# Fifteen loads move from SyncE's queue to ScalarE's, and every engine gets a new order

## The chip, the core and the metric

The kernel runs on one core of one Trainium2 chip. A core has five engines that run their own instruction streams: TensorE (PE) for matrix products, VectorE (DVE), ScalarE (ACT) and GpSimd (POOL) for everything that is elementwise or a reduction, and SyncE (SP), which here only issues transfers. Transfers are carried by 16 DMA engines. The metric is the device time of one execution in microseconds (us).

## What is computed

Attention with a forget gate over 8 batches of 8 heads (576 positions, head size 64), and behind it a bilinear feed-forward block over the 4608 tokens:

```python
scores = scale * np.matmul(q, k.transpose(0, 1, 3, 2))
cum = np.cumsum(np.log(np.clip(f, 0.0001, 1.0)), axis=-1)
scores = np.where(causal, -1000000000.0, scores + cum[:, :, :, None] - cum[:, :, None, :])
attn = np.exp(scores - np.max(scores, axis=-1, keepdims=True))
attn = attn / (np.sum(attn, axis=-1, keepdims=True) + 1e-09)
x = np.matmul(attn, v)          # then to (tokens, 512)
out = (x @ w_a) * (x @ w_b) @ w_out   # 512 -> 1536 -> 512
```

## The kernel before

The work is cut into numbered steps (`Op`, 2343 of them). Each step names an engine, or several to choose from, and a function that issues its instructions. A text called ORDER lists all steps by number, and a text called CHOICE gives one letter (D, A, P, S for DVE, ACT, POOL, SP) for each step that has a choice. The function `laid_out` (line 1096) reads both; the last loop calls the functions in that order. So each engine runs its steps in the order of ORDER, and an engine that has to wait for a semaphore holds up everything behind it on that engine. The costs in the `Op` calls are the planner's and are not read when the kernel runs.

Attention goes by t = 0 to 31, a pair of heads (two halves of 64 partitions), four t for each batch. For one t:

- `load_spread` (line 471) loads one row of the cumulated gate to 128 partitions, 576 KB into one of three buffers `spread`; step "bc" and the number t, from t = 8 on. POOL then masks two copies in it. For t = 4 to 7 TensorE spreads the row, and a copy out of PSUM (`spread_ev`, also called "bc") brings it to the buffer.
- `qk_group` (line 404) makes the scores in PSUM, `do_decay` (L520, DVE) adds the gate and takes the maximum, `do_exp` (L547, L551, ACT) takes the exponential, `do_norm` (L569, POOL) divides by the sum.
- `do_tr` (line 579) transposes the result with DMA transposes on SP's queue, "tr t A" and "tr t B" (L583, into PTA and PTB; for t = 4 to 7 A is cut into A0 and A1, which go into parts of xT). `do_pv` (L611) and `do_pv4` (L627) multiply them with v. From t = 8 on, the scores of t + 2 and the products with v of t are one step of TensorE, named by the scores ("qk").

The inputs of batch b come in seven loads (`load_v` line 239, `load_qk` line 252), here called by batch, tensor and part: k0 and q0, k1 and q1 (576 KB each), v0 and v2 (two transfers of 256 KB) and v4 (one of 128 KB). All go to one ring of three buffers, `n32`. POOL casts them to f16, TensorE transposes q and k through PSUM (`pe_transpose`, L278), and a copy by DVE or ACT (`pe_evict`) stores them as qT and kT.

The feed-forward block goes by chunks of 256, 256, 256, 384, then six of 512 tokens and a last one of 384. For each of 12 blocks of 128 columns TensorE makes psa and psb (L888, four matmuls each), ACT copies psa to f16 (`ff_copy`, L233), DVE multiplies (`ff_mul`, L899); then TensorE makes the output (L908), ACT or DVE copies it and SP stores it (L918). psa, psb, pso and the transposes of q and k share three PSUM buffers ("ff"): a fourth group can start only when the first has been copied. The feed-forward blocks are interleaved with attention, so that TensorE has work while attention waits.

Before the change SP's queue issues every load of q, k, v and spread, every DMA transpose and every store; POOL's issues the weights. In the first 20 us the gate is prepared on DVE and ACT (`clip` L177, LN L205, `scan` L180, a split into two f16 parts L209 and L185), while q and k of batch 0 are cast and transposed.

Of the kernel before, what the change touches and what calls it, by code (L numbers as in the profile page):

```python
# [25 lines left out]
def kernel(  # L26
# [212 lines left out]
    def load_v(b, sbs):  # L239
# [12 lines left out]
    def load_qk(b, which, half):  # L252
# [10 lines left out]
        nc.sync.dma_start(out=x.rearrange("p j t d -> p j (t d)"),  # L263
                          in_=src[:, 128 * half:128 * half + 128].rearrange("j p x -> p j x"))
# [38 lines left out]
    def batch_inputs(b, base):  # L303
# [7 lines left out]
        for n, (which, sbs, gm) in enumerate(order_):  # L311
            p = base - 50 + 3 * n
            gt = gate(gm)
            if which == "v":
                w, m = sbw[sbs[0]], len(sbs)
                ld = Op("SP", 0.58 * m, lambda _, sbs=sbs: load_v(b, sbs), gt, prio=p,
# [17 lines left out]
            ld = Op("SP", 0.58, lambda _, which=which, half=half: load_qk(b, which, half), gt, prio=p,  # L334
# [136 lines left out]
    def load_spread(t):  # L471

        nc.sync.dma_start(out=spread[t % RING["bc"]][:, :, SM:SM + S],
                          in_=cum_d[t:t + 1, :].to_broadcast([128, 2 * S]).rearrange("p (h s) -> p h s", h=2))
# [183 lines left out]
    def attention(t, base):  # L658
# [12 lines left out]
        if not direct:  # L671
# [11 lines left out]
            else:  # L683
                bc = Op("SP", 0.55, lambda _: load_spread(t), [o6] + last_bc[-1:], prio=prio(0) - 5, land=packets(128, 4608), lat="bc", name=f"bc{t}", bulk=True)
# [302 lines left out]
    for n in cuts:  # L987
# [3 lines left out]
        26 1 0 20 32 38 44 3 4 27 2 19 21 22 28 5 11 6 12 29 30 7 13 14 8 9 33 10 31 34 267 16 18 23-25 61 64  # L991
# [5 lines left out]
        235 108 236 249 85 250 95 90 127 1635-1637 1639 87 253 1641 128 1640 1638 133 1642 184 86 91 129 185 134  # L997
        130 1643 96 1644-1646 97 153 258 132 131 254 251 141 98 102 135 172 99 178 136 59 126 259 142 255 256
# [6 lines left out]
        342 1680 1681 343 1682 484 380 381 344 485 274 391 392 296 474 297 303 304 239 1683-1685 308 467 475  # L1005
        298-300 476 305 1686 324 486 1688 306 393 346 347 353 354 488 348 349 487 302 417 301 307 468 350 355
        1689 240 1690 1691 418 237 469 419 238 470 471 374 477 479 408 1693 1694 420 421 396 397 1695 1696
        411 412 356 403 1697-1700 352 337 395 351 330 394 480 357 338 310 1701 315 481 404 316 398 399 1702 483
        422 425 432 423 311 1703 426 400 1704 482 405 309 491 1687 493 360 358 1705 1706 427 433 406 312 439 440
        1707 1709 1711 435 1710 1708 1712 428 313 434 314 424 1713 442 1714 441 402 401 407 478 429 431 1715  # L1010
        1717 1718 446 447 1716 453 361 1719-1721 1723 454 443 533 448 1725 1722 449 1726 1727 496 345 494 1724
# [4 lines left out]
        547 554 414 532 531 461 462 556 1749 537 1751-1753 559 1754 1755 1757 1756 1759-1761 1758 560 1762 663  # L1016
        445 459 558 574 535 549 551 557 1763 1765 1764 542 1766 564 1767 1769 1768 1770 561 565 1771-1777 664
        543 544 658 550 1778 576 665 562 563 566-568 577 666 1779 1780 659 660 580 588 578 569 570 581 661 463
        1781 464 1783 465 1785 582 1784 1750 594 1782 587 1787 583 1788 590 1786 466 595 1789 1791 579 584 1790
        589 591 601 615 669 1745 670 592 571 572 667 683 674 1793 1795 1792 596 597 1794 598 1796 1797 602 1798  # L1020
        585 616 575 593 603 604 606 599 586 600 607 605 1799-1801 608 1802 671 609 618 610 1804-1806 619 622 630
        629 636 637 620 623 1807 624 672 632 673 611 612 668 684 675 1809 631 625 1810 639 638 681 613 614 725
        679 621 1811 1813-1815 643 1812 644 1817 617 640 633 1816 645 648 626 649 642 1819 1818 1820 646 647 627
        1821-1824 676 651 650 686 677 652 678 653 654 641 628 634 635 682 1825 1827 1829 690 1826 692 691 698
        704 1828 688 705 697 700 1831 1833 1830 693 706 1834 699 707 1835 1832 694 687 1836 701 689 856 656 655
        851 1803 1837-1839 711 708 712 1840 696 680 695 710 685 716 713 703 857 726 709 714 702 715 852 717
        1841-1843 1845 1844 1847 728 1849 1846 718 719 732 1848 720 1850 1851 1853 734 1854 722 721 730 739 733
        740 1852 1855 1856 746 747 1857 853 1858 1859 731 741 854 749 742 735 1860 858 748 859 860 729 855 863
        767 809 736 753 754 864 727 755 743 750 758 759 756 1862-1864 724 723 1808 1861 1867 770 1868 1869
        760 761 737 768 757 861 762 1865 745 763 764 774 788 776 790 751 738 752 789 791 792 782 772 775 781 794  # L1030
        744 1870 1872 1873 784 777 783 1874 1876 766 773 765 877 875 873 1877 1875 771 865 1878 866 867 1880
        1882 862 795 796 778 785 810 769 1879 800 797 801 1881 802-804 798 1883 786 793 780 799 787 779 805 806
# [5 lines left out]
        1051 912 902 904 881 1920-1922 913 1923 914-916 889 896 1047 922 926 934 940 927 933 924 941 903 897  # L1038
# [101 lines left out]
```

## Time and profile before

| | |
|---|---|
| median of 3 runs | 416.82 us (414.93 to 418.49) |
| the profiled execution | 417.89 us, of which 416.2 us are its span |
| granted TensorE clock, mean over the span | 0.995 |
| PE busy | 390.6 us, 94% of the span |
| DVE, ACT, POOL busy | 302.3, 278.1, 255.0 us |
| DMA moved | 80.58 MB, of 153432 packets 130720 under 512 B |

The span runs from the first to the last instruction of the profiled execution; 1.7 us of its time lie around it. Engine shares are averages over the whole span. These are the issues of transfers by line, with the size of one and the median time from issue to landing:

```profile
spread<-cum_d SPq DMA_DIRECT2D x24, 576.0 KB, 5.6
out_dram<-osb SPq DMA_DIRECT2D x36, 256.0 KB, 3.0
q<-in_q_dram SPq DMA_DIRECT2D x15, 576.0 KB, 5.7
k<-in_k_dram SPq DMA_DIRECT2D x15, 576.0 KB, 5.5
v<-in_v_dram SPq DMA_DIRECT2D x32, 256.0 KB, 5.5
...
PTB<-PB SPq DMA_TRANSPOSE x28, 5.3
PTA<-PA SPq DMA_TRANSPOSE x24, 4.2
...
xT<-PA SPq DMA_TRANSPOSE x8, 5.2
```

SPq is the queue that SP issues to. No transfer is issued by ACT.

### The profile page before, as it was taken

How to read it: one execution, taken by the hardware profiler on the slowest of the kernel's cores; microseconds unless marked ns; L12 is line 12 of the kernel's file. 1: busy time of each engine (PE TensorE's matmuls, PEld its weight loads, DVE VectorE, ACT ScalarE, POOL GpSimd, SP SyncE). 2: the span in 40 equal slices, each digit the busy share in tenths (PEclk: the TensorE clock that was granted, in tenths of full speed). 3: DMA queues.
4: the chain of work that ended last, by engine and by line, in shares of the span. 5: the costliest groups of instructions: out<-in, count | busy, mean ns of one | idle time of the engine just before them, and what ended most of it. 6: DMA issues, size and time to landing. Idle time of an engine off the chain costs nothing. (4 is left out here: it accounts for less than half of the span.)

```text
span 416.2 us, 10946 instructions
## 1 busy us (share of the span) xinstructions
PE 390.6 (94%) x3860; PEld 212.1 (51%) x3860; DVE 302.3 (73%) x1006; ACT 278.1 (67%) x790; POOL 255.0 (61%) x439
## 2 busy tenths in 40 slices
PE   1789999799998999999999999999999999999996
PEld 1456766566655544444444544444454444444552
DVE  5998998697777778867877889688877885342240
ACT  5886997685777578786878778677787773231231
POOL 7999898469477867686685586766856655000000
PEclk9999999899999999999999999999999999999999
DMA  8999999999999999999999999999966738200202
GB/s 261 240 217 237 184 223 224 180 234 195 243 247 224 285 246 194 275 229 273 235 229 245 251 253 196 230 215 292 213 138 165 162 63 173 95 0 2 101 2 76
DMA packets 153432, 80.58 MB, mean 194 GB/s; under 512 B 130720, under 2 KB 133280, under 8 KB 153376
## 3 DMA queue, kind: packets, MB, share of 16 engines
q1 hardware_dynamic: 149616, 75.15, 79.3%
q0 software_dynamic: 3760, 4.72, 6.9%
q8 instruction: 30, 0.49, 0.5%
q14 instruction: 26, 0.21, 0.2%
HBM read 52.05 MB, written 9.58 MB: 148 GB/s over the span
## 5 line engine op out<-in xcount | busy, mean ns | idle before, releaser
L520 DVE CUSTOM_DVE_ANT_0 S<-sc,spread 64x576 f32<-64x576 f32 (+4 forms) x232 | 124.9, 562 | 10.6 <-ACT PA L551 3.1
L888 PE MATMUL psb<-xT,wb 128*128 128x512 f16 (+2 forms) x528 | 116.1, 343 | 0.4 <-ACT a L233 0.4
L888 PE MATMUL psa<-xT,wa 128*128 128x512 f16 (+2 forms) x528 | 115.8, 342 | 0.3
L899 DVE TENSOR_TENSOR ht<-psb,a 128x512 f16<-128x512 f32 (+2 forms) x132 | 77.4, 589 | 34.0 <-PE psb L888 30.6
L233 ACT CAST a<-psa 128x512 f16<-128x512 f32 (+2 forms) x132 | 66.2, 502 | 51.6 <-PE psa L888 43.5
L551 ACT ACTIVATE PA<-S,st 128x256 f16<-128x256 f32 (+2 forms) x168 | 84.1, 503 | 24.2 <-DVE st L520 22.6
L908 PE MATMUL pso<-wout,ht 128*128 128x512 f16 x432 | 98.5, 379 | 0.0
L569 POOL TENSOR_SCALAR PA<-PA,st 128x384 f16<-128x384 f16 (+2 forms) x192 | 89.8, 480 | 12.4 <-DVE st L561 11.0
L569 POOL TENSOR_SCALAR PB<-PB,st 128x512 f16<-128x512 f16 (+1 forms) x96 | 67.5, 712 | 30.1 <-DVE st L561 16.4
L888 PEld LDWEIGHTS <-wb 128*128 128x128 f16 x528 | 50.1, 98 | 41.3 <-issue 1.3
L888 PEld LDWEIGHTS <-wa 128*128 128x128 f16 x528 | 49.4, 98 | 40.8 <-issue 1.8
L908 PEld LDWEIGHTS <-ht 128*128 128x128 f16 x432 | 40.6, 98 | 46.7 <-issue 0.5
L551 ACT ACTIVATE PB<-S,st 128x512 f16<-128x512 f32 x56 | 40.1, 717 | 11.7 <-DVE st L520 7.7
L410 PE MATMUL sc<-kT,qT 64*128 64x256 f16 (+5 forms) x480 | 43.7, 277 | 3.3 <-ACT PA L551 1.5
L551 ACT ACTIVATION_READ_ACCUMULATOR PA<-S,st 128x1 f32 x168 | 31.9, 190 | 0.0
L561 DVE RECIPROCAL st<-st 128x2 f32<-128x2 f32 x128 | 18.5, 158 | 18.2 <-ACT PB L551 13.1
L410 PEld LDWEIGHTS <-qT 64*128 64x128 f16 (+1 forms) x480 | 17.0, 98 | 28.2 <-issue 18.5
L486 POOL TENSOR_SCALAR_AFFINE_SELECT spread<-spread 128x256 f32<-128x256 f32 x24 | 9.8, 408 | 35.1 <-DVE st L520 35.1
L237 DVE CAST xT<-pv 128x512 f16<-128x512 f32 (+1 forms) x40 | 23.0, 575 | 8.8 <-PE pv L611 8.6
L547 ACT ACTIVATE PB<-S,st 128x576 f16<-128x576 f32 x28 | 21.8, 777 | 9.9 <-issue 6.5
L233 ACT COPY osb<-pso 128x512 f32<-128x512 f32 x19 | 10.9, 575 | 24.3 <-DMA out_dram<-osb 12.8
L520 DVE CUSTOM_DVE_ANT_1 S<-sc,spread 128x256 f32<-128x256 f32 x48 | 19.6, 420 | 9.4 <-PE sc L627 4.7
(85 smaller groups left out, 427.6 us busy)
## 6 DMA issues: line engine op xcount, KB each, us to landing
spread<-cum_d SPq DMA_DIRECT2D x24, 576.0 KB, 5.6
out_dram<-osb SPq DMA_DIRECT2D x36, 256.0 KB, 3.0
q<-in_q_dram SPq DMA_DIRECT2D x15, 576.0 KB, 5.7
k<-in_k_dram SPq DMA_DIRECT2D x15, 576.0 KB, 5.5
v<-in_v_dram SPq DMA_DIRECT2D x32, 256.0 KB, 5.5
wout<-in_moe_w_out_dram POOLq DMA_DIRECT2D x3, 512.0 KB, 6.4
v<-in_v_dram SPq DMA_DIRECT2D x8, 128.0 KB, 4.9
wa<-in_moe_w_a_dram POOLq DMA_DIRECT2D x2, 512.0 KB, 8.6
```

The source lines that it names most:

```text
L233: nc.scalar.copy(out=out_, in_=in_)
L237: VEC[e].tensor_copy(out=out_, in_=in_)
L410: nc.tensor.matmul(out=dst, lhsT=lhsT, rhs=rhs, start=start, stop=stop, skip_group_check=True)
L486: nc.gpsimd.affine_select(out=x, in_=x, compare_op=mybir.AluOpType.is_ge, fill=NEGBIG, base=0, pattern=[[0, 2], [-1, 128]], channel_multip ...
L520: nc.vector.tensor_tensor_reduce(out=o, in0=x, in1=y, scale=-1.0, scalar=3e38, op0=ADD, op1=MIN, accum_out=m)
L547: nc.scalar.activation(out=p_blocks(t, 4), in_=T[("s" if direct else "z", t, 4)], func=EXP, bias=st[:, 8:9], scale=sign, accum_out=st[:, 1 ...
L551: nc.scalar.activation(out=p_blocks(t, i)[:, :, h, :], in_=(T[("s", t, i)][:, h, :] if direct else T[("z", t, i)][:, h * n:h * n + n]).rea ...
L561: nc.vector.reciprocal(out=st[:, 20 + 2 * i:22 + 2 * i], in_=st[:, 10 + 2 * i:12 + 2 * i])
L569: VEC[e].tensor_scalar(out=p, in0=p, scalar1=st[:, c:c + 1], scalar2=1.0, op0=MUL, op1=MUL)
L888: nc.tensor.matmul(out=p[:, 0:n], lhsT=w16[:, db, 128 * fb:128 * fb + 128], rhs=xTflat[db][:, t0:t0 + n], start=(db == 0), stop=(db == 3))
L899: nc.vector.tensor_tensor(out=ht[:, 0:n], in0=T.pop(("psb", t0, fb))[:, 0:n], in1=T.pop(("a16", t0, fb))[:, 0:n], op=MUL)
L908: nc.tensor.matmul(out=o, lhsT=T[("ht", t0, fb)][:, 128 * tb:128 * tb + 128], rhs=wout16[:, fb, :], start=(fb == 0), stop=(fb == 11))
```

## The change

The three load functions take an engine and issue from that engine's queue. The steps of batch 1 and later (for k, q and v) and of t = 8 and later (for spread) may choose their engine, with ACT as one choice. The new CHOICE puts 15 of them on ACT and none on POOL: spread of t = 9, 12, 13, 17, 23, 26 and 29, and the loads k0, q1 and v4 of batch 3, k0 of batch 5, k0, q0 and v4 of batch 6, and q0 of batch 7. No DMA transpose and no store moves.

```diff
+    QUEUE = {"SP": nc.sync, "ACT": nc.scalar, "POOL": nc.gpsimd}
+
+    def load_v(e, b, sbs):
...
-            nc.sync.dma_start(out=t32[0:w, n],
-                              in_=v[b, :, 128 * sb:128 * sb + w, :].rearrange("h s d -> s h d"))
+            QUEUE[e].dma_start(out=t32[0:w, n],
+                               in_=v[b, :, 128 * sb:128 * sb + w, :].rearrange("h s d -> s h d"))
...
-                ld = Op("SP", 0.58 * m, lambda _, sbs=sbs: load_v(b, sbs), gt, prio=p,
+                ld = Op(None, {"SP": 0.58 * m} | ({"ACT": 0.72 * m + 0.1} if b else {}),
+                        lambda e, sbs=sbs: load_v(e, b, sbs), gt, prio=p,
...
-            ld = Op("SP", 0.58, lambda _, which=which, half=half: load_qk(b, which, half), gt, prio=p,
+            ld = Op(None, {"SP": 0.58} | ({"ACT": 0.8, "POOL": 0.68} if b else {}),
+                    lambda e, which=which, half=half: load_qk(e, b, which, half), gt, prio=p,
...
-                bc = Op("SP", 0.55, lambda _: load_spread(t), [o6] + last_bc[-1:], prio=prio(0) - 5, land=packets(128, 4608), lat="bc", name=f"bc{t}", bulk=True)
+                bc = Op(None, {"SP": 0.55, "ACT": 0.8, "POOL": 0.68}, lambda e: load_spread(e, t), [o6] + last_bc[-1:], prio=prio(0) - 5, land=packets(128, 4608), lat="bc", name=f"bc{t}", bulk=True)
...
     CHOICE = """
-        PDPPPPAADAADPDADAPDAPPPDDDDDAADDDDDDDDADAAADAADDDDDAAAAAAADADAAAADAAAAADDAAAAAAAAAAAAAADDAAAADAAADDA AAA
+        DPPPDPAADDADPPDAPPDDPPDDADDDAADDDDDDDDASAASAASSDASDASSDAAAAAAASAASADSSADSAAASSSASSAAASDASSDAADDSAAASS
+        SDDSADSSAASADSSSASSADASDAASSAASAASSSSSAADAAAASSAASDASASASSAASAAADDSSAASAASSSASS
     """
```

ORDER is replaced as a whole. What differs in it, by engine:

- TensorE: 96 of its 528 steps stand at another place, most of them one or two places off; 74 of the 96 are among the first 165 steps (roughly the first 110 us), 22 behind.
- 24 steps other than the loads change engine. Of batch 0: the first half of k's cast goes from POOL to DVE, the second part of q's first cast from ACT to DVE, the second part of k1's cast from DVE to POOL, the first part of q1's from ACT to POOL, and v4's from POOL to DVE. Three copies of spread rows (t = 4 and 5) go from DVE to ACT. From batch 3 on, six copies of transposed q and k go from ACT to DVE, one the other way.
- DVE starts with the clip of the second half of the gate (which waits for the gate's load) ahead of its casts of q; before, it cast q first.
- SP's transposes keep their sequence but for exchanges of neighbours (tr8A ahead of tr8B, for one); loads and stores move between them.

More of the change, by code (lines that the diff above doesn't have):

```diff
@@ L250, in cast_v, with load_qk @@
         cast(e, nv[b % 2][0:w, sbs[0]:sbs[0] + n].rearrange("p n h d -> p n (h d)"), t32[0:w, 0:n], False)
-    def load_qk(b, which, half):
+    def load_qk(e, b, which, half):
         if b == 0 and half:
@@ L262, in load_qk @@
         src = src_of[which][b].rearrange("(j h) (g t) d -> j (h g) (t d)", j=2, t=TG)
-        nc.sync.dma_start(out=x.rearrange("p j t d -> p j (t d)"),
-                          in_=src[:, 128 * half:128 * half + 128].rearrange("j p x -> p j x"))
+        QUEUE[e].dma_start(out=x.rearrange("p j t d -> p j (t d)"),
+                           in_=src[:, 128 * half:128 * half + 128].rearrange("j p x -> p j x"))
     def cast_qk(e, b, which, half, lo, hi):
@@ L469, in spread_tail, with load_spread @@
         nc.gpsimd.memset(spread[t % RING["bc"]][:, :, SM + SF:SM + S], 0.0)
-    def load_spread(t):
-        nc.sync.dma_start(out=spread[t % RING["bc"]][:, :, SM:SM + S],
-                          in_=cum_d[t:t + 1, :].to_broadcast([128, 2 * S]).rearrange("p (h s) -> p h s", h=2))
+    def load_spread(e, t):
+        QUEUE[e].dma_start(out=spread[t % RING["bc"]][:, :, SM:SM + S],
+                           in_=cum_d[t:t + 1, :].to_broadcast([128, 2 * S]).rearrange("p (h s) -> p h s", h=2))
     def mask_copy(t):
@@ L1016 @@
[L1016 to L1020, printed above, removed]
@@ new lines @@
+        226 60 221 287 263 288 222 264 472 231 232 385 335 384 1671 323 194 233 1673 1672 334 1675 373 293
+        339 340 329 1674 386 266 381 281 473 295 336 331 380 388 294 330 338 389 390 484 234 1676 341 1677 1679
+        342 1680 1681 1678 195 343 1682 274 485 392 391 474 1683-1685 303 296 393 297 475 298 299 304 300 476
+        417 387 301 302 1686 305 324 239 240 306 307 467 308 468 344 486 346 347 353 488 348 354 487 1688-1690
[5 rows of a table added]
+        1724 498 1725-1727 499 505 1728 506 512 513 456 450 1729 500 1730 501 1731 1733 1735 365 1734 507 1736
@@ new lines @@
+        366 1732 508 497 437 444 534 430 438 457 452 445 509 519 520 495 510 415 1737 1739 1741 489 359 514 515
+        662 573 1742 490 502 416 1738 524 525 1740 521 522 526 527 363 536 1743 516 538 528 552 553 545 539 364
+        451 530 511 523 517 518 503 504 540 409 458 1692 460 657 1746-1748 547 541 546 548 1744 531 461 462 537
+        413 1751 1749 559 554 555 1752 1753 1755 1757 1756 549 560 1754 556 542 1758 1759 529 532 1760 561 1761
+        1763 1764 414 1762 1765 1767 1768 535 663 564 562 1766 1769 551 544 669 459 667 558 557 1770 543 550 658
@@ new lines @@
+        574 1771 1773 566 1772 1774 565 1775-1777 664 576 1778 665 567 666 577 568 580 659-661 582 569 563 1779
+        463 1780 1781 594 587 570 464 581 1782 588 578 1783 465 1785 1787 1784 583 1789 590 589 1788 595 1786
+        579 1791 1793 597 1792 584 1790 466 591 601 1794 596 598 602 1745 615 571 674 1795 1796 603 683
+        1797 1798 572 1750 585 670 586 593 575 606 607 604 616 592 600 1799-1801 671 609 1802 608 672 618 610
+        622 629 1804-1806 630 636 620 637 623 1807 624 632 673 631 605 599 612 611 668 1809 625 1810 638 639
[3 rows of a table added]
@@ new lines @@
+        700 707 856 656 655 851 1803 1835 689 1836 694 711 1837-1839 712 1840 726 682 685 696 695 713 708 714
[3 rows of a table added]
+        768 727 758 743 759 750 1862-1864 760 761 1867 770 1868 1869 738 737 745 756 757 762 764 763 774 772 788
[3 rows of a table added]
+        1887 1888 1890 825 832 1889 826 819 833 815 1892-1894 1891 837 834 820 838 839 827 1895 1896 1898 1900
+        876 811 842 808 807 1866 868 843 813 1897 844 845 1899 1901-1903 840 836 874 828 821 919 880 884 891
+        1045 841 835 822 829 869 1904 882 898 899 846 885 892 848 847 886 1905 1906 1908 1910 893 900 894 1909
@@ new lines @@
+        887 901 1907 895 1911 883 870 905 902 872 881 888 906 871 1050 1871 1912 1914 1916 1913 1918 1917 907
+        1915 896 903 1051 879 897 904 1046 889 910 1919 911-913 849 850 1920-1922 1047 1923 920 914 915 890 922
+        1048 926 934 940 961 916 962 1049 1055 928 924 941-943 936 927 908 909 933 935 929 944 946 1925-1927
+        1052 925 1053 1928 947 930 931 1054 937 948 949 921 952 953 950 923 939 945 954 955 938 932 1056 951
+        1930 1931 1924 917 918 1929 1932 1935-1937 964 1940 956 1938 1933 1942 966 968 975 982 969 983 976 958
[9 rows of a table added]
@@ new lines @@
+        1134 1135 1118 1128 1117 1110 1109 1091 1097 1083 1098 1084 1156 1247 1248 1122 1129 1123 1998-2001 1241
+        1119 1242 1130 1137 1243 1136 1251 1997 1112 2003-2005 1111 2008 2010 1141 1142 1115 1143 1138 1146 1124
+        1147 2006 1131 1148 1149 2009 1150 1152 1126 2012 1158 2011 1144 1162 1160 1145 1133 1151 1197 1139 1125
+        1163 2013 2014 1159 2015 1140 1252 1132 1164 2016 2018 1176 2017 1165 2020 1170 1177 1169 1178 1171 2021
+        1179 2022 2019 1172 1166 2023-2025 1256 1265 1266 1161 1253-1255 1154 1183 1184 1180 1257 1168 1157 1198
@@ new lines @@
+        1182 1167 1153 1249 2026 2027 1188 1189 1173 1175 1181 1174 2028 2029 1185 2030 2031 1186 1258 1200 1259
+        1191 1190 1260 2032 2034 2036 1204 1202 1192 1212 1205 1211 1218 1219 1201 1187 1193 1206 1263 2033
+        1207 1208 2035 1194 2037 1214 1213 1203 1215 1225 2038 2039 1250 2040-2042 2044 2046 2002 1307 1195 1196
+        2007 1261 1226 1220 1221 2043 2048 1222 1216 1199 1230 2045 1227 1308 1224 1217 1223 1209 1231 1228 2047
+        1232 2049 1233 1234 2050 1268 2052 2051 1272 1286 1287 1279 1280 1270 1269 1274 2053 1288 2054 2055 1264
@@ new lines @@
+        1229 1236 1235 1273 1281 1289 1275 1438 1282 2056-2059 1290 1210 1292 1433 1271 1293 1294 1262 1267 1291
+        2061 1238 1237 2060 1349 1295 2062 2063 1283 1276-1278 1285 1434 1298 1296 1299 2064 1301 1300 1302 1303
+        1284 1297 1304 2066-2069 1435 1310 1312 1314 1315 1328 1322 1329 1321 1311 1439 1350 2065 1443 1316
+        1436 1437 2071-2073 1440 1313 2074 1331 1317 1324 1330 1323 1441 2076 2077 1442 1335 1336 2078 2080
[5 rows of a table added]
+        2113 2070 1445 1387 1375 1390 1389 1412 1406 1396 1399 1395 1405 1413 1401 1408 2114 1446 1407 2116-2118
[3 rows of a table added]
@@ new lines @@
+        1432 1431 2133 1448 1543 2128 2134-2136 1487 1488 1461 1502 1489 1492 1493 1484 1494-1496 1490 1449 2139
+        1504 2140 2141 1472 1477 1486 1491 1497 1505 1508 1522 1479 1498 1544 1478 1471 1485 1516 1523 1515 1509
+        1506 2137 1510 2144 1525 1518 1511 2145 1517 1524 2146 1507 2142 2147 1529 2148-2150 2152 2154 1500 1499
[4 rows of a table added]
+        1596 1580 1597-1599 2181 1574 1603 1594 1604 1610 2182 1611 2183 2184 1605 1612 2185 1606 1613 1600 1561
+        2186 1595 1607 1569 1575 1582 1581 1555 1602 1609 1570 2187 1617 1562 1563 1618 2188-2190 1614 2191 1619
@@ new lines @@
+        1601 1591 1622 1620 1616 1615 1608 1624 1623 1625 1626 1593 2192 2193 1584 1583 1629 2194 2195 1627 1621
+        1628 2197 2198 1587 2199 1588 2202 1585 2203 2204 2200 1586 2207 1630 2196 2201 2205 2208 1631 2209 1632
+        2210 2206 2211-2214 2216 2218 2215 2217 2219-2224 2226 2228 2225 2227 2229-2232 2234 2233 2235 2236 2238
+        1633 2237 2239-2242 1634 2243-2246 2248 2249 2247 2250-2252 2254 2253 2255 2256 2258 2260 2261 2257 2259
+        2262 2265-2268 2270 2263 2269 2264 2271 2272 2275 2273 2276-2278 2274 2280 2282 2281 2284 2283 2286 2285
@@ L1094 @@
+        SDDSADSSAASADSSSASSADASAASSAASAASSSSSAADAAAASSAASDASASSASSAAADDSSAASAASSSASS
     """
```

65 lines of the change are left out of this document (6 added, 59 removed), and 82 rows, old and new, of the table ORDER.

## The prediction

> **What bounds the kernel now.** I read the slices of the page first, to see whose time it is.
>
> ```profile
> PE   1789999799998999999999999999999999999996
> ...
> PEclk9999999899999999999999999999999999999999
> DMA  8999999999999999999999999999966738200202
> ```
>
> One slice is 10.4 us. PE stands at 9 from about 145 us to its last matmul: what that part takes is TensorE's own work, and the change adds no work there. Only the start (the first two slices), the stretch from 60 to 145 us and one dip of the clock (eighth slice of PEclk) can give anything back. The tail is fixed: the timeline has the last output matmul end at 412.2 us, then a copy and a store to 416.2. So the question is how long PE idles before 145 us, and whether anything new stops it later. The waits of PE say for whom it idles:
>
> ```profile
> PE psT L278 <- DVE q L235: 5.4, 1, 5.4
> PE pv L611 <- DMA xT<-PA: 3.5, 3, 2.5
> PE psT L278 <- POOL k L237: 3.2, 2, 2.8
> PE pv L611 <- DMA PTA<-PA: 1.7, 2, 1.0
> ...
> PE psT L278 <- DVE ht L899: 1.4, 1, 1.4
> ...
> PE pv L627 <- DMA PTB<-PB: 0.5, 1, 0.5
> ...
> PE psb L888 <- ACT a L233: 0.4, 1, 0.4
> ```
>
> Columns: us in total, times, longest. The first and third are the start. Behind it, the waits for a transpose are the large ones: 3.5 + 1.7 + 0.5 = 5.7 us; asked stretch by stretch, these six lie at 69, 71, 81, 97, 107 and 140 us, none later. ACT, which is to get the loads, hardly holds PE: 0.4 us for the copy of psa. The longest of them has a price beyond itself, by the windows of 1 us (PE busy, PEld, DVE, ACT, POOL, then the granted clock, DMA share, GB/s):
>
> ```profile
> 79.00:80.00 1.00, 0.00 (x0) 0.00 (x0) 0.59 (x2) 0.00 (x0) 0.80 (x1) 1.00 1.28 287
> 80.00:81.00 1.00, 0.01 (x2) 0.01 (x2) 0.00 (x0) 0.56 (x1) 0.00 (x0) 0.77 1.12 152
> 81.00:82.00 1.00, 1.00 (x9) 0.70 (x10) 0.00 (x0) 0.26 (x2) 0.00 (x0) 0.50 1.12 290
> 82.00:83.00 1.00, 1.00 (x7) 0.69 (x6) 0.40 (x1) 0.00 (x0) 0.00 (x0) 0.50 0.99 207
> 83.00:84.00 1.00, 1.00 (x7) 0.70 (x6) 0.94 (x4) 0.56 (x2) 0.00 (x0) 0.53 1.16 231
> ```
>
> After 2.5 us of idle PE runs at half clock for 2.9 us: 1.5 us more, 4.0 in all. By the Trainium skill, "TensorE: Matmul & The Clock Gate", section "Why this matters for your kernels", gaps beyond about 3 us drop the clock; here 2.5 was enough, so I go by the row.
>
> Why are the transposes late? The timeline of SP's queue (start, us it took to issue):
>
> ```profile
> 71.90 5.21 SPq L583 DMA_TRANSPOSE PTB<-PB  x1
> 77.21 1.76 SPq L583 DMA_TRANSPOSE xT<-PA  x1
> 79.06 0.54 SPq L473 DMA_DIRECT2D spread<-cum_d  x1
> ...
> 118.66 6.68 SPq L583 DMA_TRANSPOSE PTA<-PA  x1
> ```
>
> The transpose that PE wants at 81 us is the one issued at 77.21, behind one whose issue took 5.21. Adding the pieces, SP issues during 59.5 of the 63 us from 62 to 125 (94%), and 111 of the 190 us from 160 to 350 (58%). A transpose takes 1.2 to 6.7 us to issue (median 1.8), though the DMA share is at 1.05 to 1.19 in every 20 us up to 220: the engines are full too, not only the queue.
>
> **The loads leave SP.** Six of the 15 lie in the full stretch: bc9, k0, q1, v4 of batch 3, bc12 and bc13. Their issues on SP took 0.54, 0.58, 0.47, 0.65, 0.82 and 0.95 us, 4.0 in all. The bytes stay, at nearly the same place among TensorE's steps (bc9 12 steps earlier, the others within 3). What the queue gives back wait by wait: the two at 69 and 71 us (0.8) come before any moved load: nothing. At 81 us (pv5), SP's sequence ahead of the transpose is as it was, but one psb of 256 tokens now stands ahead of pv5, which covers 0.44; bc9, now issued before and not behind that transpose, could take it away again. At 97 (0.72) one spread and one store fewer stand ahead: half, 0.36. At 107 (1.0) tr8A now goes before tr8B and without k0 ahead: all of it. At 140 (0.67) bc13 is gone but two loads remain ahead: half, 0.34. Sum 2.1; bounds: 7.2 (all 5.7 and the half clock) and -4.0 (a new wait like that at 81). I take 2.1, as the engines' share says that most of the lateness is bytes. By the Trainium skill, "DMA: Bandwidth & Descriptors", section "Issuing engines are not separate DMA queues", another issuing engine saves only sequencer time, since all transfers share the 16 engines; the ceiling would then be the 4.0 us of issue rather than 7.2. The full DMA slices agree with it.
>
> **The loads come to ACT.** No row has a transfer issued by ACT. Nearest are SP's issues of the same loads: 0.36 to 2.45 us for spread (mean 0.71), 0.37 to 3.03 for q and k (mean 0.70). Behind the issue in ACT's order stand exponentials and the copies of psa, which free the three PSUM buffers for PE. Cover: in the chunks of 256 tokens a group takes 0.44 us and the copy 0.37, so a copy may come 2 x 0.44 - 0.37 = 0.5 late; with 384, 2 x 0.65 - 0.475 = 0.8; with 512, 2 x 0.864 - 0.577 = 1.15. The six loads above fall in chunks of 256 and 384, the other nine in 512. At 0.7 with exponentials close by I charge the six 0.25 each, 1.5 us, and the nine nothing. Bounds: 0, and 15 x 0.7 = 10.5 if the cover is gone everywhere. Each load also waits on ACT for its buffer. For most, the last reader stands over 40 steps earlier; close are k0 of batch 5 (a POOL cast 7 steps before), bc29 (9) and v4 of batch 3 (14).
>
> **Other choices from batch 3 on.** Five net copies of q and k leave ACT (0.63 each) for DVE (0.75): 3.8 us more on DVE, spread over some 100 us in which it is busy 14 to 18 of every 20. No gain, as ACT isn't PE's bound; cover on DVE 2 us or more per 20; without it, at most 3.8. I take 0.
>
> **The start.** Here the new order can be followed by hand.
>
> ```profile
> 4.83 0.49 DVE L235 TENSOR_SCALAR q<-q 128x512 f16<-128x512 f32 x1 [2.57 <-DMA q<-in_q_dram]
> 5.82 1.02 DVE L177 TENSOR_SCALAR cum_f<-cum_f 96x256 f32<-96x256 f32 x2 [0.49 <-DMA cum_f<-in_f_dram]
> 11.89 1.02 DVE L494 TENSOR_REDUCE st<-sc 128x2 f32<-128x512 f32 x2
> ```
>
> DVE now begins with a clip, which cannot start before 5.82, and casts q behind it. Up to the first maximum it has, by the rows: clips 0.72 + 0.38, q 0.50 and, scaled by columns, 0.62, likewise k 0.70, scans 0.67 + 0.88, splits 0.80 + 0.55 + 0.42, one copy of qT 0.75: 7.0 us from 5.82, so 12.8 against 11.89. POOL gets k1 and q1 casts between the splits (0.84 each): q1 is ready at about 15.8, and its transposes stand in TensorE's order ahead of the next scores, which began at 14.79 and now at about 16.6; the step after, at 16.38 before, follows at some 17.3. I charge 1.0; bounds 0 (the full DVE and ACT of 40 to 60 us then get 2 us less on DVE, as spread copies go to ACT) and 1.8.
>
> **Sum.** On the profiled execution: 417.9 + 1.0 + 1.5 - 2.1 = 418.3. It lay 1.1 above the median, so 417.2 for the median.
>
> **Rivals.**
>
> 1. *The queue was the limit* (faster). If transposes are late because loads stand ahead in SP's queue and not for bytes, all waits behind 71 us and the half clock go: 5.7 - 0.8 + 1.5 = 6.4, and ACT's price stays in its cover: 417.9 + 1.0 - 6.4 = 412.5, 411.4 in the median; without the start's loss 410.4. For: SP 94% full exactly where PE waits. Against: DMA share above 1.
> 2. *ACT waits for SP's issue* (slower). If the two queues' issues exclude each other, a load on ACT meets SP issuing in 94% of cases early and 58% late, and waits half of a median issue of 1.8 us before its own 0.5: 1.4 us. Over the cover (0.5 and 1.15) this is 0.9 x 6 x 0.94 + 0.25 x 9 x 0.58 = 6.4 us for PE: 417.9 + 1.0 + 6.4 - 1.1 = 424.2, if the transposes gain nothing. It decides once a load stays over 1 us on ACT. For: SP's own issues grow to 6.7 us. Against: no row shows two queues at once. The Trainium skill, "Perfetto Trace Analysis", section "DMA Instruction — HWDGE (DVE, Sync)", says that the generator of descriptors is locked for exclusive use during an issue; this trace cannot show whether across queues.
> 3. *A new long wait* (slower): bytes of ACT's queue now compete with SP's transposes, the old waits stay, and one more is as long as that at 81 us, 4.0 with the half clock: 417.2 + 2.1 + 4.0 = 423.3. For: bc9 now comes before the transpose of pv5. Against: the order of TensorE leaves most transposes as much lead as before.
> 4. *Nothing moves but the order*: the loads are issued where they were, bytes bind, and only the start is lost: 417.9, within the forecast's range.
>
> **How the numbers follow.** My forecast with rival 4: 0.35, nearly all within 1% of 416.8 (412.7 to 421.0; the three runs of before spread over 0.9%, so less than 1% is little to tell from no change): 0.30 within, 0.02 faster, 0.03 slower. Rival 1: 0.30, of which 0.26 faster, 0.04 within. Rival 2: 0.23, 0.21 slower, 0.02 within. Rival 3: 0.12, 0.10 slower, 0.02 within. So faster 0.28, within 0.38, slower 0.34. The forecast's own range is 413 to 421; with rival 1 down to 409.5 and rival 2 up to 425.5 about 0.2 is left out.
>
> **What would show it.** Start: the first maximum on DVE at 12.8 and not 11.9. Loads: rows of ACT's queue with a mean near 0.7 (over 1.0 speaks for rival 2), and PE's wait for ACT's copy at 1 to 2 us, not 0.4. Transposes: PE's waits for DMA at 3 to 4 us, the half clock still there; both gone means rival 1. SP's share from 62 to 125 us should fall to about 88%. PE waiting for ACT or DVE behind 160 us would make the prediction wrong.

## The result, and the profile after

The change makes the kernel slower: 423.91 us (median of 4 runs, 422.77 to 424.94) against 416.80 (4 runs) on the same chip, a ratio of 1.016, 95% interval 1.0125 to 1.0195. The profiled execution took 422.77 us, its span is 421.1, 4.9 more than before. All ratios below are to the kernel before on the same chip, with 95% intervals, and leave disturbed runs out; three of the profiles below (e4, e6, e13) are of longer executions than their medians, with TensorE waiting 2.4 to 4.9 us for weights near 35 us, and are used only for single transfers and waits, not for their length.

The slices of the page of after, to be laid beside those of before:

```profile
PE   1789998759989999999999999989999999999996
...
PEclk9999999969999999999999999999999999999999
DMA  8799999998999999999999999996977827300102
```

PE is again full from about 145 us on. The loss lies ahead: the eighth and ninth slices (73.7 to 94.8 us) read 7 and 5, where before they read 7 and 9, and the dip of the clock has moved to the ninth. The waits of PE in after (us in total, times, longest):

```profile
PE psT L280 <- DVE q L235: 7.9, 1, 7.9
PE pv L615 <- DMA xT<-PA: 7.6, 3, 6.3
PE sc L414 <- ACT PA L555: 1.7, 3, 0.8
PE pv L615 <- DMA PTB<-PB: 1.5, 1, 1.5
...
PE pv L615 <- DMA PTA<-PA: 0.9, 1, 0.9
...
PE pso L912 <- ACT osb L233: 0.4, 1, 0.4
```

Lines have moved by four (L611 is now L615, L583 is L587). The waits for a transpose were 5.7 us in all and are 10.0. Asked stretch by stretch, those of before at 97 and 140 us are gone and that at 107 has shrunk from 1.0 to 0.2; that of pv5 has grown from 2.5 to 6.3 (82 to 88 us), and two are new (1.5 near 124 us, 0.9 near 278). The windows of 1 us about the long one (PE, PEld, DVE, ACT, POOL, then clock, DMA share, GB/s):

```profile
81.00:82.00 1.00, 1.00 (x10) 0.68 (x7) 1.00 (x5) 1.00 (x6) 1.00 (x2) 1.00 0.26 61
82.00:83.00 1.00, 0.05 (x1) 0.00 (x0) 0.99 (x4) 0.26 (x2) 1.00 (x3) 1.00 1.44 178
83.00:84.00 1.00, 0.00 (x0) 0.00 (x0) 0.97 (x3) 0.00 (x0) 1.00 (x2) 1.00 1.22 97
84.00:85.00 1.00, 0.00 (x0) 0.00 (x0) 0.15 (x1) 0.00 (x0) 0.30 (x1) 0.88 0.85 186
...
87.00:88.00 1.00, 0.00 (x0) 0.00 (x0) 0.00 (x0) 0.20 (x1) 0.00 (x0) 0.50 1.26 199
88.00:89.00 1.00, 0.65 (x7) 0.42 (x8) 0.07 (x1) 1.00 (x3) 0.00 (x0) 0.50 1.27 290
```

PE stands, then DVE, ACT and POOL run dry behind it, and the clock is halved from about 84.8 us until about 91.6. At 81 to 82 us, where tr5B has been issued, tr5A0 is being issued and neither has landed, the DMA engines are busy at 0.26. So here it is not bytes that the transposes wait for. The lull alone isn't what is new: at 77 to 78 us in before the share was 0.46 with 30 GB/s, and in e3 below it is 0.13 with 43 GB/s at 78 to 79 us, also with tr5B not yet landed. What differs is what comes after it. SP's queue at that place (start, us to issue), then ACT's one transfer there:

```profile
74.33 0.39 SPq L477 DMA_DIRECT2D spread<-cum_d  x1
74.82 3.57 SPq L587 DMA_TRANSPOSE PTB<-PB  x1
78.47 3.66 SPq L587 DMA_TRANSPOSE xT<-PA  x1
82.23 5.41 SPq L587 DMA_TRANSPOSE PTB<-PB  x1
```

```profile
75.78 0.39 ACTq L477 DMA_DIRECT2D spread<-cum_d  x1
```

ACT's load is bc9 (the spread load of t = 9), issued 0.96 us into SP's issue of tr5B, with 2.6 us of that issue still to come; tr5A0, which pv5 waits for, follows at once. From the trace's landings and packets, beside those of before:

```
               before                         after
tr5B           71.90 issued, 80.34 landed     74.82 issued, 87.70 landed
tr5A0          77.21 issued, 80.95 landed     78.47 issued, 88.31 landed
bc9            79.06 issued, 83.94 landed     75.78 issued, 87.52 landed   (SP before, ACT after)
```

ACT is done with the issue after 0.39 us, but the first packet of its queue starts at 82.05, when SP's issue of tr5A0 ends (82.13). From there to 86 us the 256-byte packets of SP's queue come at 56 to 436 per us; in e3 below, in which these two transposes run undisturbed, they come at 1051 and 1022 per us (79 to 81 us). All three transfers land together, 10 to 13 us after their issue.

How late TensorE is against before, by the start of the same feed-forward matmul in both traces (a count from the traces, us):

```
at (before)   33    77    86    101   131   181   290   412
after         2.5   3.1   7.4   6.3   5.4   4.2   5.6   5.0
```

So 2.5 us were lost before 33 us and 4.3 more at pv5; 3.2 came back by 181 us, where before had its own waits from 97 to 140 us; 1.4 went again by 290 us.

Two more lines of the page of after, the issues by queue with the median time to landing:

```profile
spread<-cum_d SPq DMA_DIRECT2D x17, 576.0 KB, 5.6
...
spread<-cum_d ACTq DMA_DIRECT2D x7, 576.0 KB, 7.9
```

The same load takes 2.3 us longer to land from ACT's queue, in this kernel's mixture of places.

### The profile page after: what moved, and what is told of

It reads as the page before. It is cut to its first block, busy times and chain, and to the rows that moved or that the text cites. A ratio compares the mean times of both kernels' runs of the same rounds, so it can differ in the third digit from the quotient of the medians.

```text
span 421.1 us, 10948 instructions
## 1 busy us (share of the span) xinstructions
PE 391.6 (93%) x3860; PEld 212.3 (50%) x3860; DVE 304.0 (72%) x1009; ACT 277.7 (66%) x787; POOL 253.9 (60%) x439
## 5 line engine op out<-in xcount | busy, mean ns | idle before, releaser
L524 DVE CUSTOM_DVE_ANT_0 S<-sc,spread 64x576 f32<-64x576 f32 (+4 forms) x232 | 125.0, 562 | 10.1 <-PE sc L414 4.9
L573 POOL TENSOR_SCALAR PA<-PA,st 128x256 f16<-128x256 f16 (+2 forms) x192 | 89.5, 479 | 18.9 <-DVE st L565 15.1
L237 DVE CAST xT<-pv 128x512 f16<-128x512 f32 (+1 forms) x40 | 23.1, 576 | 12.8 <-PE pv L615 12.7
L615 PEld LDWEIGHTS <-nv 128*64 128x64 f16 x640 | 19.6, 110 | 17.7 <-issue 10.1
```

Source lines behind the costliest of these rows:

```text
L237: VEC[e].tensor_copy(out=out_, in_=in_)
L524: nc.vector.tensor_tensor_reduce(out=o, in0=x, in1=y, scale=-1.0, scalar=3e38, op0=ADD, op1=MIN, accum_out=m)
L573: VEC[e].tensor_scalar(out=p, in0=p, scalar1=st[:, c:c + 1], scalar2=1.0, op0=MUL, op1=MUL)
L615: nc.tensor.matmul(out=o[HP[h], 128 * i:128 * i + 128], lhsT=vt[:, j, pr + NP * h, :], rhs=pt[:, base_blk[i] + 2 * block_at(t, i, j) + h, ...
```

## The experiments

The two theories that the first four kernels were to tell apart: **A**, a load on ACT's queue that falls into SP's issue of a DMA transpose holds up both (queue and place together); against it, that the new order alone, the fifteen issues on ACT by their number, or the new start is what costs. In the diffs, 533 is bc9, 493 bc8, 360 tr5B, 358 tr5A0, 410 tr6B, 405 and 603 exponentials of t = 6 and t = 10, 674 the load q1 of batch 3, 683 bc12.

**e1: the new order, all loads on SP.**

```diff
 CHOICE, the fifteen moved loads, at their new places in ORDER
-A
+S
```

> The new order with all 15 loads issued by SP, at the places that they have in the new order. Theory A (the queue: spread of t = 9, issued early by ACT, is carried beside tr5B and tr5A0 and holds them up): PE's wait for the transpose of pv5 falls from 6.3 us to below 3 and the half clock shortens, so about 419 to 420 us. Theory B (the order: start and sequence make the wait, whoever issues the loads): the wait stays at 5 us or more and the time at 422 to 425.

**e2: the old order, the fifteen loads on ACT.**

```diff
 CHOICE of before, the fifteen loads, at their old places in ORDER
-S
+A
```

> The old order and the old choices, but the 15 loads issued by ACT at their old places, where spread of t = 9 comes behind tr5A0. Theory A with the early issue as its condition, and theory B: 416 to 418, as before. If loads on ACT cost by themselves (PE waiting for ACT's copies), 420 or more, with PE's waits for ACT above 3 us where they were 0.9 behind the start.

**e3: after, with bc9 alone at another place,** still on ACT.

```diff
 ORDER of after
-491 1687 493 360 533 1706 1707
+491 1687 493 360 1706 1707
-1721 1723 410 449
+1721 1723 410 533 449
```

> The changed kernel with one step moved: spread of t = 9, still on ACT, behind tr6B in the order and so behind six more exponentials and four more copies on ACT. Theory A: tr5B and tr5A0 land some 5 us after their issue and not 10 to 13, PE's wait falls from 6.3 us to 3 or less, and the time to 419 to 420. Theory B: the wait stays, 423 to 424.

**e4: the first 130 steps in the old order and on the old engines,** the rest as after.

> The changed kernel with its first 130 steps (to about 20 us) in the old order and with the old choices, the rest in the new order. The first maximum on DVE comes back from 13.3 to 11.9 us and the first psa from 35.5 to about 33.5. If the late start is carried to the end: 421.5 (2.4 less). If idle time behind absorbs it: 423.5. By theory A the wait for pv5 stays at about 6 us; by theory B it may fall with the start.

Measured:

```
            median (runs)    ratio   95% interval      longest wait for a transpose
after       423.91 (4)       1.016   1.0125 to 1.0195  6.3, xT, 82 us
e1          419.11 (10)      1.006   1.003  to 1.0094  2.8, PTB
e2          424.51 (4)       1.018   1.013  to 1.023   5.4, PTB, 116 us
e3          416.82 (10)      0.999   0.9954 to 1.0026  1.5, PTB
e4          423.45 (4)       1.014   1.0093 to 1.0193  7.5, xT, 86 us
```

e3 moves one step of 2343 and gives the whole loss back: 7.1 us in the medians, 2 to 3 us more than theory A expected. In its trace ACT issues bc9 at 80.99, when SP is just ending tr6B's issue, and the load lands at 86.12, after 5.1 us. The waits of PE in e3:

```profile
PE pv L615 <- DMA xT<-PA: 2.0, 3, 1.1
...
PE pv L615 <- DMA PTB<-PB: 1.5, 1, 1.5
...
PE pv L615 <- DMA PTA<-PA: 0.9, 1, 0.9
```

The wait at pv5 is down to 1.1 and the granted clock is 1.00 from 79 to 92 us. e1 says that the new order by itself costs 2.6 us, and that with SP as the issuer bc9's early place makes no such wait: at pv5 it is 2.4 us. e4 gives nothing back that can be measured: the start isn't the loss. (It also moved the weights' loads, and its profile has TensorE wait 3.4 us for them, so as a price of the start it is no more than that.)

e2 was the surprise. In the old order bc9 stands behind tr5A0, and pv5 waits only 1.2; the loss is the same size, but at another load. The queue of SP, and what ACT issued beside it:

```profile
108.56 4.67 SPq L587 DMA_TRANSPOSE PTB<-PB  x1
113.28 4.19 SPq L246 DMA_DIRECT2D v<-in_v_dram  x2
```

```profile
109.47 0.37 ACTq L477 DMA_DIRECT2D spread<-cum_d  x1
...
109.95 0.41 ACTq L265 DMA_DIRECT2D q<-in_q_dram  x1
```

bc12 and q1 come 0.9 and 1.4 us into SP's issue of tr9B. Their first packets start at 113.75, half a microsecond behind its end, and they land 10.75 and 12.26 us after issue; PE waits for that transpose:

```profile
PE pv L615 <- DMA PTB<-PB: 5.4, 1, 5.4
```

The same pattern with other steps, then, in another order. The next kernels took it apart.

**e5: the order of before, bc9 alone on ACT and early.**

```diff
 ORDER of before (and CHOICE: bc9 from S to A)
-405 309 491 1687 493 360 358
+405 309 491 1687 493 533 360 358
-443 533 448
+443 448
```

> The order and the choices of before, with one step changed: the spread load bc9 is issued by ACT behind the exponential of t = 6 (at about 74.4 us), while SP issues tr5B (71.9 to 77.1 in before). All other loads stay on SP. Theory A (a load on ACT's queue that is issued while SP issues a DMA transpose starts its packets only when that issue ends, and then both crawl): bc9 and tr5A0 land 10 us or more after their issue, PE waits 5 us or more for xT at about 82 us with the half clock behind it, 420.5 to 424 us. Rival (it takes the full set of loads on ACT, or the new order with its earlier bc9): 416 to 418 us, PE's longest wait for xT stays near 2.5.

**e6: the order of before, bc9 early but on SP,** between the two transposes.

```diff
 ORDER of before
-493 360 358
+493 360 533 358
-443 533 448
+443 448
```

> The order and the choices of before, with bc9 still on SP but one place earlier: between tr5B and tr5A0. Theory A: SP issues it by itself, so nothing crawls; tr5A0 is issued some 0.6 us later, 416.5 to 418.5 us, wait for xT at 81 us between 2.5 and 4. Rival (the place of the bytes ahead of tr5A0 is what costs, on whichever queue): 420 us or more, with a wait for xT of 5 us or more.

e5: 421.70 us (4 runs from 419.65 to 433.82; without the longest, 419.96), 1.0123 (1.0046 to 1.0201). e6: 419.34 (10), 1.0048 (1.0013 to 1.0083). ACT's issue of bc9 in e5 and SP's queue about it:

```profile
73.69 0.39 ACTq L477 DMA_DIRECT2D spread<-cum_d  x1
```

```profile
72.53 3.10 SPq L587 DMA_TRANSPOSE PTB<-PB  x1
75.72 2.77 SPq L587 DMA_TRANSPOSE xT<-PA  x1
78.60 5.96 SPq L587 DMA_TRANSPOSE PTB<-PB  x1
```

bc9's first packet starts at 78.57, again with the end of tr5A0's issue (78.49). bc9 lands 10.8 us after its issue, tr5B 12.2 and tr5A0 9.5. Of PE's waits in e5 between 79 and 92 us there is one:

```profile
PE pv L615 <- DMA xT<-PA: 5.4, 1, 5.4
```

With the profile of e2, in which bc9 is on ACT at its old place, this gives pv5's wait for all four combinations:

```
bc9        old place (behind tr5A0)   early (beside or between the transposes)
on SP      2.5 (before)               2.3 (e6), 2.4 (e1)
on ACT     1.2 (e2)                   5.4 (e5), 6.3 (after)
```

The two of the new order are e1 and after, the others of the old. Neither the queue nor the place does it; the two together do. In time e6 was 1 to 3 us dearer than expected, and the intervals of e5 and e6 overlap, so it is the waits that tell them apart, and of the times the pair after and e3.

**e7: e2 with bc12 and q1 of batch 3 some 17 steps later.**

```diff
 ORDER of before (CHOICE as in e2)
-592 571 572 667 683 674 1793
+592 571 572 667 1793
-616 575 593 603 604
+616 575 593 603 683 674 604
```

> The order of before with the fifteen loads on ACT (the kernel that measured 424.51), but bc12 and q1 of batch 3 are issued by ACT some 17 steps later, behind the exponentials of t = 10, when SP should have ended the issue of tr9B. Theory A: the wait of 5.4 us for PTB at 120 us goes and the time falls to 416 to 419.5 us. Rival (fifteen issues on ACT cost by their number, wherever they fall): 423 us or more.

**e10: e2 with these two back on SP,** at the places of before.

```diff
 CHOICE of e2, bc12 and q1 of batch 3
-A
+S
```

> The order of before with thirteen of the loads on ACT; bc12 and q1 of batch 3 stay on SP at their places of before (with all fifteen on ACT this order measured 424.51; with these two some 17 steps later it measured 421.42, but ACT then issued them at 112.73 and 113.21, at the very end of SP's issue of tr9B, 109.08 to 113.13, and its runs lay between 417.1 and 423.9). Theory A (these two cost what that kernel lost): 416 to 419 us, and no wait of 2 us or more for PTB near 120 us. Rival (it takes no particular load; thirteen issues on ACT cost by their number): 421 us or more.

Both expectations failed in time: e7 took 421.42 (10 runs from 417.08 to 423.88), 1.0085 (1.0048 to 1.0122), and e10 423.44 (4), 1.0159 (1.0124 to 1.0193). The profiled execution of e7 took 417.20 us, near the lowest of its runs, and has no wait over 1.0 us for a transpose; what the longer ones wait for isn't seen. bc12 was issued at 112.73, 0.4 us ahead of the end of tr9B's issue, so that the separation hung on a fraction of a microsecond. e10's trace is plain. SP's queue (x2 stands for two transposes), ACT's load beside it, and ACT some 12 us later:

```profile
92.63 10.02 SPq L587 DMA_TRANSPOSE PTB<-PB  x2
```

```profile
92.84 0.43 ACTq L265 DMA_DIRECT2D k<-in_k_dram  x1
```

```profile
105.07 0.77 ACT L551 ACTIVATE PB<-S,st 128x576 f16<-128x576 f32 x1 [1.85 <-DMA PTB<-PB]
```

Here k0 of batch 3 has fallen into the first transpose's issue (3.84 us of the 10.02), 0.2 us behind its start. It lands after 11.9 us and the transpose after 12.3, at 104.96. The exponential that needs the transpose's source buffer back waits 1.85 us on ACT, the copy of psa queues behind it, and PE waits for that copy:

```profile
PE psb L892 <- ACT a L233: 2.1, 2, 1.7
```

Later v4 of batch 3 falls into the issue of tr10B in the same way (1.25 of its 4.18 us are over), that transpose lands after 10.1 us, and PE waits 2.1 us for PTB near 133 us; v4 itself took only 7.0 us.

In e2 k0 at the same place was issued 0.09 us ahead of that transpose (91.60 against 91.69) and landed after 5.7 us. So what was wrong in the expectation was not the mechanism but that two named loads carry it: in the old order several of the fifteen lie at the edge of a transpose's issue, and small shifts decide which one falls in. The rival, that ACT pays by the number of loads, has the time of e10 right, but e3 and the next kernel have all fifteen on ACT at 416.8 and 415.5.

Over all fourteen profiles, in the stretch from 60 to 160 us, the 39 of 47 loads on ACT whose landing the traces give, by what was left of SP's running transpose issue when ACT issued them (a count from the traces):

```
left of the issue       loads   us from issue to landing
2.3 us or more            6     7.0, 10.7, 11.7, 11.9, 12.3, 13.0
under 2.3 us             14     4.1 to 7.5, and one of 10.8 (e5, a second transpose directly behind)
no transpose in issue    19     4.4 to 7.4
```

The bound of 2.3 us was chosen with these numbers in sight. Transposes with a load of ACT in their issue landed after 7.5 us in the median (16 of them, the slowest 13.8), the others after 5.2 (229, three quarters of them within 6.3, the slowest 10.9: tr5B of e13 below, with a load of POOL in its issue). A transpose whose issue is long both lands late and is likelier to meet a load. So among those with 3 us or more of issue: 7 with a load of ACT landed after 12.2 us in the median (7.1 to 13.8), 59 without after 7.2. Behind 160 us no load on ACT took over 9.8 us, and PE's queue of feed-forward work covers it but for 0.9 us in after (2.1 in e11).

**e9: after with three edits:** bc9 as in e3, q1 of batch 3 out of tr9B's issue, and q's casts on DVE ahead of the clip that waits for the gate.

```diff
 ORDER of after (besides that of e3)
-26 0 1 20 32 38 44 3 11 4 27 28 5
+26 0 1 20 32 38 44 3 27 28 11 4 5
-615 571 674 1795 1796 603 683 1797
+615 571 1795 1796 603 683 674 1797
```

> The kernel after the change with three edits: bc9 behind tr6B (as in the run that measured 416.82), q1 of batch 3 behind bc12 (out of SP's issue of tr9B), and DVE casts q ahead of the clip that waits for the gate's load. Theory A with a start that costs about 1 us: 414 to 415.8 us, so under both kernels; the wait of 1.5 us for PTB near 120 us goes, and the first maximum on DVE comes at about 12 us. Rival (the start's order is hidden by the full DVE and ACT from 40 to 60 us, and the wait for PTB moves elsewhere): 416 to 418 us.

**e12: the order of e9, all loads on SP.**

```diff
 CHOICE of e9, the fifteen loads
-A
+S
```

> The order of the kernel that measured 415.54 (all three edits), with the fifteen loads on SP at the same places. If the queue's time is worth what the prediction gave it (4.0 us of issue in the full stretch, of which 2.1 reach TensorE at most): 416.5 to 418.5 us. Rival (what the kernel gains over the one before comes from the order alone): 414.5 to 416.3 us.

**e11: e9 with the first 130 steps of before.**

> The first 130 steps in the order and with the engines of before; behind them the order after the change with bc9 behind tr6B and q1 of batch 3 behind bc12. If the new start costs the 1.0 to 1.5 us by which TensorE lags at 33 us in the run that measured 415.54: 413.5 to 414.8 us, under both kernels. Rival (the full engines of 40 to 60 us take it back, or the old start holds up the weights' loads): 415.5 to 418 us.

```
            median (runs)    ratio   95% interval
e9          415.54 (10)      0.998   0.9956 to 1.001
e12         419.48 (8)       1.007   1.0043 to 1.0095
e11         416.20 (12)      0.996   0.993  to 0.9991
```

ACT's two loads in e9 and SP's transpose ahead of them:

```profile
114.09 0.39 ACTq L477 DMA_DIRECT2D spread<-cum_d  x1
...
114.60 0.41 ACTq L265 DMA_DIRECT2D q<-in_q_dram  x1
```

```profile
109.53 4.37 SPq L587 DMA_TRANSPOSE PTB<-PB  x1
114.00 0.53 SPq L922 DMA_DIRECT2D out_dram<-osb  x1
```

Both now come behind the issue, land after 4.5 and 7.2 us, and the wait for PTB (1.5 in e3) is gone; PE's waits for transposes add up to 3.1 us. In e12, with the same order and SP as the issuer, that wait is back:

```profile
PE pv L615 <- DMA PTB<-PB: 2.4, 1, 2.4
```

e9 against e12 is the price of the queue with the order held fixed: 0.9%, or 3.6 us (1.0069 - 0.9983, times 416.8), in favour of ACT; by the two intervals about 2 to 5 us. The expectation of e12 failed: 419.48 lies above both of its ranges, so the queue's time is worth more than the sum gave it. So the change's move of loads does bring something once no load falls into a transpose's issue, and the new order takes 0.6 to 0.7% back (e1, e12). e9 and e11 are 1.8 and 2.0% faster than after. Against before, e11 is 0.1 to 0.7% faster by its interval, which is at the edge of what can be told; the interval of e9 contains 1. The old start makes no difference between the two that can be measured.

**e13: the order of before, bc9 alone on POOL's queue.**

```diff
 ORDER of before (and CHOICE: bc9 from S to P)
-441 402 401 407
+441 402 533 401 407
-443 533 448
+443 448
```

> The order and the choices of before with bc9 alone moved to POOL's queue, issued at about 75 us, while SP issues tr5B and tr5A0 (the same load on ACT at 73.7 us measured 421.70, on SP between the two transposes 419.34). If any second queue does it: 420.5 us or more, a wait for xT of 5 us or more at 82 us, bc9 landing 10 us or more behind its issue. If it is ACT's queue alone: 416 to 419.5 us, the wait for xT at 3 us or less.

418.28 us (10 runs from 415.21 to 422.96), 1.0012 (0.9978 to 1.0046). POOL was late and issued bc9 at 78.79, 0.7 us ahead of the end of tr5B's issue, and not in its midst. In the profiled execution, 422.96 us long, tr5B landed after 10.9 us and PE waited 5.0 for xT; the median says that this is not the rule. Whether any second queue does what ACT's does stays open.

## Why the prediction came out as it did

The forecast was 417.2 us, with a range of its own of 413 to 421 and, with the rivals, of 409.5 to 425.5; its likeliest case was no change (0.38). The time lies outside the forecast's own range and inside the wide one, as slower (0.34). Of the cases named, rival 3 came nearest, which had been given 0.12; so the wide range held, and the sum did not.

- **What bounds the kernel** was right: TensorE's idle time ahead of 145 us decided, and behind it no more than 1.4 us were lost. The sign that was to make it wrong, PE waiting for ACT or DVE behind 160 us, came to 0.9 us in all (0.2 before).
- **The transposes, -2.1: the step that failed, at one of its terms.** "At 81 us (pv5)" the sum took a gain of 0.44, and added that bc9, "now issued before and not behind that transpose, could take it away again". It took away far more: the wait went from 2.5 to 6.3, so this term is +3.8 where -0.44 stood. I had seen that bc9's place was new, gave it nothing in the sum, and kept it for the bound and for rival 3, as bytes ahead of a transpose. As bytes on SP it would indeed have cost nothing at pv5 (2.3 in e6, 2.4 in e1). What was not priced is what e5 shows: the same load, at this place, on the other queue. The other terms came: at 97, 107 and 140 us the waits fell by 0.7, 0.8 and 0.7, 2.2 in all where 1.7 was taken. The new waits of 1.5 and 0.9 us were not foreseen. Instead of 5.7 - 2.1 = 3.6 us, PE waits 10.0 us for transposes, 4.3 more than before.
- **The bounds of that term** were -7.2 to +4.0, the upper one from a new wait like that at 81 us. Of the two halves that made it, the wait is 3.8 us longer, and the half clock costs what it cost before: it now lasts 6.8 us and not 3.4, but a good half of it lies in the wait, and PE runs about 3 us at it in both.
- **ACT's price, 1.5,** was about 0. The issues take 0.37 to 0.69 us, none is held, and PE's wait for a copy of psa (0.4 before) is not among the waits of after. The cover that was worked out was enough. Of the signs named, their mean (0.43, where near 0.7 was expected) spoke against rival 2, and SP's share from 62 to 125 us fell further than to 88%, to 76% (48.0 of 63 us), partly because SP too ran dry.
- **The start, 1.0,** was 2.5 in the profiled execution. The first maximum on DVE came at 13.31 and not at 12.8, because the gate's load, for which DVE now waits first, landed later here:

```profile
7.22 0.32 DVE L177 TENSOR_SCALAR cum_f<-cum_f 96x320 f32<-96x320 f32 x1 [4.96 <-DMA cum_f<-in_f_dram]
...
13.31 1.00 DVE L498 TENSOR_REDUCE st<-sc 128x2 f32<-128x512 f32 x2
```

  In before DVE could start on it at 5.82, in e3 at 6.47, here at 7.22, so the step was right about what DVE waits for and took one execution's landing for a fixed number. But with q cast first (e9), and with the whole old start (e11), TensorE is still 1.6 us late at 33 us; that part lies behind step 130 and was not in the sum. How much of it reaches the end wasn't told apart: e4 and e11 gained nothing measurable.
- **Rival 1** (the queue is the limit) is half true and was hidden by rival 3: with the order fixed, the queue is worth 3.6 us (e9 against e12), more than the 2.1 of the sum, and less than the 6.4 of the rival. The sum argued that "most of the lateness is bytes". The measured price is close to the 4.0 us of issue that the six early loads took on SP. By the Trainium skill, "DMA: Bandwidth & Descriptors", section "Issuing engines are not separate DMA queues", another issuing engine saves only the time on the sequencer; e9 and e12 agree with that as a size. The section also has all transfers interleave whichever engine started them; here the packets of ACT's queue did not start for 6.3 us, at the end of which the DMA engines stood at 0.26, so in this stretch they did not interleave; later they did (82 to 86 us), at the slow rate given above.
- **Rival 2** (ACT waits for SP's issue) had the wrong victim. The two queues do get in each other's way while SP issues a transpose, but ACT goes on after 0.39 us; it is the load's first packet that comes late, in two traces together with the end of SP's issue of the next transpose (82.05 against 82.13 in after, 78.57 against 78.49 in e5). That it waits for this end is not shown: in e4 bc9's first packet started 3.0 us after its issue, 1.4 us ahead of the end of tr5B's issue (82.11 against 83.53), and the load still took 13.0 us, tr5B 13.8. In e9, where no transpose was in issue, bc9's came 1.9 us after its issue (82.73 against 80.83). So the late start is not the whole cost; the slow packets behind it stand in e4 too. By the Trainium skill, "Perfetto Trace Analysis", section "DMA Instruction — HWDGE (DVE, Sync)", the generator of descriptors is locked during an issue. The late first packets of after and e5 would fit a generator shared by both queues, but that of e4 came while SP was still issuing. No run here separates this from other causes, and the slow packets afterwards (transposes at half their rate or less until the load is through) are not explained by it.
- **Rival 3** gave 423.3 and its reason "bytes of ACT's queue now compete with SP's transposes", with the right place and the right transpose. Its time is right to 0.6 us, partly by chance: the old waits did go, and the start cost more. Its mechanism is right as far as the queue goes; that the load has to fall into SP's issue of a transpose is from e3, e5 and the count by what was left of the issue. Why the packets then come so slowly stays open.

Three readings in the prediction are slightly off and move nothing in its result: the DMA share of before was 0.86 in the first 20 us, SP's issues of spread took 0.65 us in the mean and not 0.71, and its issues from 160 to 350 us fill 107 us and not 111 once the gaps within joined rows are left out.

## What to carry to other kernels

When a load moves from one queue to another, the question is not only what the old queue gains but what it is issuing at the moment when the load goes out: here a load that fell on ACT while SP had 2.3 us or more of a DMA transpose's issue left landed, with the transpose, 10 to 13 us after its issue in five cases of six, and one such load cost the kernel 7 us. Place such loads behind an issue of a long transpose, by the traces of the kernel that is to run, and leave more than a few tenths of a microsecond, since which load collides changed with small shifts (e2, e7, e10). Hold the order fixed when the value of a queue is asked: the move itself was worth 3.6 us, and the order and one place hid it.

## What was not expected of the hardware

- A transfer issued on ACT in 0.39 us had its first packet 6.3 us later, across two issues of transposes on SP that followed each other within 0.1 us, while, in the last of these 6.3 us, the DMA engines were at 0.26 of their time and moved 61 GB/s.
- The time to issue one and the same transpose differs from kernel to kernel (tr5B: 5.21 us before, 3.57 after, 3.10 in e5), so a position in the order doesn't fix what a load on the other queue meets.
- The clock halved some 2.7 us into the wait of after (at about 84.8, PE's last work before it at 82.05) and some 2.0 us into that of before (at about 80.5, by the share of 0.77 in its window of 80 to 81 us; PE stood from 78.5). The length of the wait alone doesn't tell: after one of 2.4 us in e1 the clock halved, after one of 2.3 us in e6 it did not.
